# Layer one's weights shared by halves between the first two token blocks, and conversion work moved off GpSimd

## The chip, the core and the metric

The kernel runs on one core of one Trainium2 chip. The metric is device microseconds of one execution, the median of several. The engines are called TensorE (PE in the profile, PEld its weight loads), VectorE (DVE), ScalarE (ACT), GpSimd (POOL) and SyncE (SP, here the queue that issues every DMA).

## What is computed

A decayed linear attention (4 batches, 8 heads, 576 positions, head size 64) is followed by two feed-forward layers over 2304 tokens, 512 wide inside and 2048 in the middle. The weights come as float64, everything else as float32, and the products keep float32's digits.

```python
def _attn_ref(q, k, v):
    scores = np.matmul(q, k.transpose(0, 1, 3, 2)) / np.sqrt(64)
    Dmat = np.where(rel >= 0, gamma[:, None, None] ** rel[None, :, :], 0.0)
    return np.matmul(scores * Dmat[None], v)

def reference(**kwargs):
    x = attn_out.transpose(0, 2, 1, 3).reshape(2304, 512)
    h = x @ moe_w_in
    x = np.where(h > 0, h, np.exp(np.minimum(h, 0)) - 1) @ moe_w_out
    h = np.maximum(x @ moe2_w_in, 0)
    return (h * h) @ moe2_w_out
```

## The kernel before

**Products.** Every float32 operand is held as a pair of float32r parts, hi and lo. `split` (L99) makes the pair: ScalarE casts hi (L101) and a second engine subtracts to get lo (L102). `mm3` (L104) issues three matmuls for each product, hi by hi, hi by lo and lo by hi (L105 to L107).

**Blocks and steps.** The tokens go in five blocks, four of 512 and one of 256. A step is one block and one f of 16, that is 128 of the 2048 middle columns. `up` (L270) computes h in 12 matmuls into one of two PSUM banks, takes the nonlinearity in three ScalarE instructions and two VectorE ones (`t` at L287, the max at L288), and splits g. `down1` (L296) adds that f's share into four PSUM banks `acc`, 12 matmuls, and runs LAG = 2 steps behind. Layer one runs all 16 f of block zero, then of block one, and so on; layer two follows in the same manner, reading layer one's outputs back from DRAM.

**Weights.** A unit is 128 columns of w_in or 128 rows of w_out; a layer has 32 units, two for each f. `load_raw` (L112) fetches a unit's float64 words, 512 KB, into one of three buffers `raw`. `to_f32` (L124) makes float32 of them. ScalarE scales the lower words in place (L131) and takes the magnitude of the upper words (L132), VectorE does min (L133), shift (L134) and sign (L135), and GpSimd adds the rounded lower words (L138). `split_w` (L149) then makes the pair, with the subtraction on GpSimd for layer one's w_out and on VectorE otherwise. Layer one's pairs stay in SBUF, each under a tag of its own, through all five blocks. `w1_step` (L372) loads, splits and converts one unit per count; it is called once with each of the first block's attention pieces and twice in each step until all 32 units are done. From step 16 on, layer two's units are converted at 0.7 per step, parked in DRAM and fetched back in layer one's last block.

**Attention.** It runs by chunks of at most 128 positions: `transposes`, `scores`, `values`. `scale_chunk` (L179) multiplies q and k by their decays, on GpSimd for blocks zero and one and on VectorE for the rest. Block zero's four chunks come first, three of them in places of weights that come late. The attention of each later block is spread over the steps of the block ahead of it (`mid`, L404), since a block's first up-step needs its whole x.

**Order.** Each engine runs its instructions in the order that a scheduler fixes when the program is built. The scheduler takes what the program issues first, among what its own model holds ready. All DMAs go through SP's one queue, in order.

## Time and profile before

| what | value |
|---|---|
| median of 3 runs | 928.61 us (928.36 to 928.87) |
| span of the profiled execution, first to last instruction | 926.7 us |
| TensorE busy | 895.6 us, 97% |
| VectorE busy | 488.0 us, 53% |
| ScalarE busy | 420.5 us, 45% |
| GpSimd busy | 138.0 us, 15% |
| mean granted TensorE clock | 0.992 of full speed |

The profile shows one execution; its own time is the span, and the median of the runs is 1.9 us above it. Busy shares are averages over stages that differ much, so the stages have to be read apart: the attention of block zero (to about 35 us), the steps of block zero with the conversion of layer one's weights (to about 159 us), and all that follows. Busy times of matmuls overlap each other, since the ends of pipelined matmuls are modelled; a group's matmuls therefore add up to more than the time they took.

### The profile page before, as it was taken

How to read it: one execution, taken by the hardware profiler on the slowest of the kernel's cores; microseconds unless marked ns; L12 is line 12 of the kernel's file. 1: busy time of each engine (PE TensorE's matmuls, PEld its weight loads, DVE VectorE, ACT ScalarE, POOL GpSimd, SP SyncE). 2: the span in 40 equal slices, each digit the busy share in tenths (PEclk: the TensorE clock that was granted, in tenths of full speed). 3: DMA queues.
4: the chain of work that ended last, by engine and by line, in shares of the span. 5: the costliest groups of instructions: out<-in, count | busy, mean ns of one | idle time of the engine just before them, and what ended most of it. 6: DMA issues, size and time to landing. Idle time of an engine off the chain costs nothing.

```text
span 926.7 us, 12546 instructions
## 1 busy us (share of the span) xinstructions
PE 895.6 (97%) x4934; PEld 741.2 (80%) x4934; DVE 488.0 (53%) x784; ACT 420.5 (45%) x762; POOL 138.0 (15%) x102
## 2 busy tenths in 40 slices
PE   6988788999999999999999999999999999999997
PEld 4766566878888888999888888888888888988886
DVE  4799999676656655776566542232223222323222
ACT  4576676665556565665666532222222222222221
POOL 4565555121111111211000000000000000000000
PEclk9999999999999999999999999999999999999999
DMA  9752555274434533663443420030002002100001
GB/s 227 180 159 93 159 150 158 65 230 127 113 100 173 137 91 107 220 176 122 150 126 92 159 91 1 1 137 1 0 1 91 1 1 82 55 2 23 1 1 45
DMA packets 94778, 89.09 MB, mean 96 GB/s; under 512 B 59008, under 2 KB 77568, under 8 KB 94208
## 3 DMA queue, kind: packets, MB, share of 16 engines
q1 hardware_dynamic: 94720, 88.30, 32.2%
q8 instruction: 38, 0.62, 0.3%
q14 instruction: 20, 0.16, 0.1%
HBM read 65.74 MB, written 22.54 MB: 95 GB/s over the span
## 4 chain that ended last, share of the span: by engine, by line
PE 83%; DVE 11%; issue 2%; ACT 1%; DMA 1%; POOL 1%; SPq 0%; DVEq 0%; ACTq 0%
PE acc L105 13%; PE acc L106 13%; PE acc L107 13%; PE h L105 13%; PE h L106 13%; PE h L107 13%; DVE f L133 2%; DVE f L135 2%; DVE t L287 2%; PE ps_o L242 2%; DVE f L134 1%; PE ps_s L223 1%; PE ps_t L210 1%; PE ps_o L238 1%; DVE w L102 1%
## 5 line engine op out<-in xcount | busy, mean ns | idle before, releaser
L105 PE MATMUL h<-x,w 128*128 128x512 f32 (+1 forms) x640 | 238.3, 373 | 6.5 <-DVE t L288 5.8
L107 PE MATMUL h<-x,w 128*128 128x512 f32 (+1 forms) x640 | 237.8, 372 | 1.9 <-DVE w L102 1.9
L106 PE MATMUL h<-x,w 128*128 128x512 f32 (+1 forms) x640 | 237.1, 371 | 0.0
L292 DVE SCALAR_TENSOR_TENSOR t<-h,t 128x512 f32<-128x512 f32 (+1 forms) x80 | 51.1, 639 | 229.9 <-ACT t L290 229.9
L290 ACT ACTIVATE t<-h 128x512 f32<-128x512 f32 (+1 forms) x80 | 44.5, 556 | 237.1 <-PE h L107 237.1
L101 ACT CAST g<-t 128x512 fp32r<-128x512 f32 (+1 forms) x160 | 92.4, 578 | 128.0 <-DVE t L288 65.2
L105 PEld LDWEIGHTS h<-x,w 128*128 128x128 f32 x640 | 121.3, 190 | 29.8 <-ACT e L284 3.8
L102 DVE TENSOR_TENSOR g<-t,g 128x512 fp32r<-128x512 f32 (+1 forms) x160 | 108.7, 679 | 66.3 <-ACT g L101 59.4
L107 PEld LDWEIGHTS h<-x,w 128*128 128x128 f32 x640 | 121.2, 189 | 24.7 <-DVE w L102 4.4
L106 PEld LDWEIGHTS h<-x,w 128*128 128x128 f32 x640 | 121.4, 190 | 21.1 <-DVE x L102 0.4
L138 POOL TENSOR_TENSOR f<-f,raw 128x512 int32<-128x512 int32 x64 | 94.2, 1472 | 270.6 <-DVE f L135 186.1
L106 PE MATMUL acc<-g,w 128*128 128x512 f32 (+1 forms) x320 | 119.3, 374 | 2.5 <-DVE g L102 2.5
L105 PE MATMUL acc<-g,w 128*128 128x512 f32 (+1 forms) x320 | 116.8, 381 | 4.9 <-ACT g L101 4.8
L107 PE MATMUL acc<-g,w 128*128 128x512 f32 (+1 forms) x320 | 118.1, 370 | 0.0
L105 PE MATMUL acc<-w,g 128*128 128x512 f32 x288 | 112.2, 390 | 0.0
L106 PE MATMUL acc<-w,g 128*128 128x512 f32 x288 | 112.2, 390 | 0.0
L107 PE MATMUL acc<-w,g 128*128 128x512 f32 x288 | 111.6, 389 | 0.0
L287 DVE SCALAR_TENSOR_TENSOR t<-e,t 128x512 f32<-128x512 f32 (+1 forms) x80 | 60.0, 750 | 53.6 <-ACT t L285 53.1
L105 PEld LDWEIGHTS acc<-g,w 128*128 128x128 f32 x320 | 60.0, 190 | 16.9 <-ACT g L101 5.7
L283 ACT ACTIVATE t<-h 128x512 f32<-128x512 f32 (+1 forms) x80 | 44.3, 554 | 60.6 <-PE h L107 59.6
L106 PEld LDWEIGHTS acc<-g,w 128*128 128x128 f32 x320 | 60.5, 189 | 13.8 <-DVE g L102 4.0
L107 PEld LDWEIGHTS acc<-g,w 128*128 128x128 f32 x320 | 60.4, 189 | 10.1
(62 smaller groups left out, 954.8 us busy)
## 6 DMA issues: line engine op xcount, KB each, us to landing
raw<-in_moe_w_in_dram SPq DMA_DIRECT2D x32, 512.0 KB, 4.2
raw<-in_moe_w_out_dram SPq DMA_DIRECT2D x32, 512.0 KB, 3.6
x2s<-x SPq DMA_DIRECT2D x16, 512.0 KB, 3.3
w2s<-f SPq DMA_DIRECT2D x32, 256.0 KB, 2.3
f<-w2s SPq DMA_DIRECT2D x32, 256.0 KB, 2.7
x<-x2s SPq DMA_DIRECT2D x4, 2048.0 KB, 7.9
out_dram<-o SPq DMA_DIRECT2D x18, 256.0 KB, 2.1
q<-in_q_dram SPq DMA_DIRECT2D x13, 256.0 KB, 4.3
```

The costliest lines, as they stand in the source:

```text
L101: nc.scalar.copy(pair_hi, src)
L102: eng.tensor_tensor(out=pair_lo, in0=src, in1=pair_hi.bitcast(F32), op=ALU.subtract)
L105: nc.tensor.matmul(ps, l_hi, r_hi, start=first, stop=False)
L106: nc.tensor.matmul(ps, l_hi, r_lo, start=False, stop=False)
L107: nc.tensor.matmul(ps, l_lo, r_hi, start=False, stop=last)
L133: nc.vector.tensor_scalar_min(a, a, MOST)
L135: nc.vector.scalar_tensor_tensor(out=ai, in0=upper, scalar=-(1 << 31), in1=ai, op0=ALU.bitwise_and, op1=ALU.bitwise_or)
L138: nc.gpsimd.tensor_tensor(out=ai, in0=ai, in1=lower, op=ALU.add)
L283: nc.scalar.activation(t, h, AF.Relu, scale=-1.0)
L287: nc.vector.scalar_tensor_tensor(out=t, in0=e, scalar=1.0, in1=t, op0=ALU.add, op1=ALU.mult)
L290: nc.scalar.activation(t, h, AF.Relu)
L292: nc.vector.scalar_tensor_tensor(out=t, in0=h, scalar=0.0, in1=t, op0=ALU.max, op1=ALU.mult)
```

## The change

- **Halves.** Layer one's steps run in the order f 0 to 7 of block zero, f 0 to 7 of block one, f 8 to 15 of block zero, f 8 to 15 of block one, and then blocks two to four as before. A half's four sums are copied from PSUM to SBUF by ScalarE and written to DRAM (`parts`). At the end of the second half they are loaded back into raw buffers and added by VectorE before the split.
- **Spread.** The attention of block one now lies in steps 0 to 6, that of block two in steps 24 to 30.
- **Raw words.** Layer one's raw units load into the place that their pair will take, so each has a place of its own; `w1_step` issues loads up to six units ahead of the conversion. Layer two's still use the three `raw` buffers, which the halves' sums share.
- **GpSimd.** The rounding add and the split of layer one's w_out go to VectorE, and so does the scaling of block one's chunks. GpSimd keeps the scaling of block zero's chunks. The add is built as a custom VectorE instruction over 1024 half-words per partition.

Comments were taken out as well; those lines are left out of the diff.

```diff
+AHEAD = 6
+HALF = NF // 2
+ORDER1 = [(b, h * HALF + f) for h in range(2) for b in range(2) for f in range(HALF)]
+ORDER1 += [(b, f) for b in range(2, NB) for f in range(NF)]
+SPREAD = {1: (0, HALF - 1), 2: (3 * HALF, 4 * HALF - 1), 3: (2 * NF, 3 * NF - 3), 4: (3 * NF, 4 * NF - 3)}
...
+    parts = dram.tile([2, P, KC, TB], F32, tag="parts", name="parts")
...
-        t = raw_p.tile([P, DM, 2], I32, tag="raw", name="raw")
+        if layer == 0:
+            t = wp.tile([P, DM, 2], I32, tag=f"w{which}_{f}", name="raw")
+        else:
+            t = raw_p.tile([P, DM, 2], I32, tag="raw", name="raw")
...
-        nc.gpsimd.tensor_tensor(out=ai, in0=ai, in1=lower, op=ALU.add)
+        nc.vector.tensor_tensor(out=ai, in0=ai, in1=lower, op=ALU.add)
...
-        split(t[:, 0], t[:, 1], f32s.pop(u), nc.gpsimd if which and layer == 0 else nc.vector)
+        split(t[:, 0], t[:, 1], f32s.pop(u))
...
-        eng = nc.gpsimd if ch in blocks[0] + blocks[1] else nc.vector
+        eng = nc.gpsimd if ch in blocks[0] else nc.vector
...
+    def halves(blk):
+        return blk < 2
...
+        half = halves(blk)
+        first, last = f == 0 or half and f == HALF, f == NF - 1 or half and f == HALF - 1
+        if first:
             acc_t[blk] = [ps_acc.tile([P, TB], F32, tag="acc", name=f"acc{m}") for m in range(KC)]
+        if f == NF - 1 and half:
+            back = [raw_p.tile([P, 2, TB], F32, tag="raw", name="part") for _ in range(KC // 2)]
+            for i, t in enumerate(back):
+                nc.sync.dma_start(out=t, in_=parts[blk, :, 2 * i:2 * i + 2])
...
             if f == NF - 1:
+                if half:
+                    t = back[m // 2][:, m % 2]
+                    nc.vector.tensor_tensor(out=t, in0=a, in1=t, op=ALU.add)
+                    a = t
...
+            elif last:
+                if m % 2 == 0:
+                    part = raw_p.tile([P, 2, TB], F32, tag="raw", name="part")
+                nc.scalar.copy(part[:, m % 2], a)
+                if m % 2:
+                    nc.sync.dma_start(out=parts[blk, :, m - 1:m + 1], in_=part)
...
-            step("raw", 99, w1, lambda u: load_raw(*u))
+            while at["raw"] < min(at["f32"] + AHEAD, len(w1)):
+                step("raw", 99, w1, lambda u: load_raw(*u))
             step("split", at["f32"], w1, split_w)
-            step("f32", at["raw"] - 2, w1, to_f32)
+            step("f32", at["raw"], w1, to_f32)
...
-    steps = [(0, blk, f) for blk in range(NB) for f in range(NF)]
+    steps = [(0, blk, f) for blk, f in ORDER1]
...
+            for of, (lo, hi) in SPREAD.items():
+                if lo <= i < hi:
+                    need = 3 * len(blocks[of])
+                    for _ in range((i - lo + 1) * need // (hi - lo) - (i - lo) * need // (hi - lo)):
+                        attn_step()
...
-                while at["raw"] == len(w1) and at["f32"] < len(w1) and at["f32"] < 2 * i + 6:
-                    step("f32", 99, w1, to_f32)
```

The built order shows where the instructions now stand. First VectorE, in before: from one step's t to the next one's in the early part of block zero (`L287` t, `L288` max, `L133` to `L135` a conversion, `w_2` the split of a unit of f 2, `g` the split of a step's result).

```order
L287 SCALAR_TENSOR_TENSOR t<-e,t 128x512
L288 TENSOR_TENSOR t<-h,t 128x512
L102 TENSOR_TENSOR w_2_268<-f,w_2_268 128x512
L133 TENSOR_SCALAR f<-f 128x512
L102 TENSOR_TENSOR x<-ps_o,x 128x4x64
L134 TENSOR_SCALAR f<-f 128x512
L102 TENSOR_TENSOR g<-t,g 128x512
L135 SCALAR_TENSOR_TENSOR f<-raw,f 128x512
L287 SCALAR_TENSOR_TENSOR t<-e,t 128x512
L288 TENSOR_TENSOR t<-h,t 128x512
L133 TENSOR_SCALAR f<-f 128x512
L134 TENSOR_SCALAR f<-f 128x512
```

VectorE in the changed kernel, between the eighth step of block zero and the first step of block one (`L146` to `L148` and `ISA` at L151 are a conversion with its add, `L111` splits, `L239` and `L271` attention).

```order
L148 SCALAR_TENSOR_TENSOR f<-raw,f 128x512
L147 TENSOR_SCALAR f<-f 128x512
L151 ISA f<-raw,f 128x1024
L146 TENSOR_SCALAR f<-f 128x512
L148 SCALAR_TENSOR_TENSOR f<-raw,f 128x512
L147 TENSOR_SCALAR f<-f 128x512
L111 TENSOR_TENSOR w_12_1160<-f,w_12_1160 128x512
L151 ISA f<-raw,f 128x1024
L111 TENSOR_TENSOR x<-ps_o,x 128x4x64
L148 SCALAR_TENSOR_TENSOR f<-raw,f 128x512
L271 TENSOR_TENSOR st<-ps_u,st 64x4x64 x2
L146 TENSOR_SCALAR f<-f 128x512
```

In before each few conversions are followed by a step's t, max and g; in the changed kernel there is a stretch with conversions and attention alone, 74 instructions long, and the last split of block one's x (`x<-ps_o,x 128x4x64`) stands inside it.

TensorE in before, in the middle of block zero (`h` is an up-step, `acc` a down-step, `ps_t` the transposes of a chunk of the next block).

```order
L105 MATMUL acc_698<-g,w_5_550 128x512
L106 MATMUL acc_698<-g,w_5_550 128x512
L107 MATMUL acc_698<-g,w_5_550 128x512
L105 MATMUL h<-x,w_8_669 128x512
L106 MATMUL h<-x,w_8_669 128x512
L210 MATMUL ps_t<-cs,q 128x128 x4
L105 MATMUL acc_695<-g,w_6_613 128x512
L105 MATMUL acc_696<-g,w_6_613 128x512
L107 MATMUL h<-x,w_8_669 128x512
L105 MATMUL h<-x,w_8_669 128x512
```

TensorE in the changed kernel, at the end of block zero's first half.

```order
L115 MATMUL acc_762<-g,w_7_746 128x512
L116 MATMUL acc_762<-g,w_7_746 128x512
L115 MATMUL acc_763<-g,w_7_746 128x512
L116 MATMUL acc_763<-g,w_7_746 128x512
L223 MATMUL ps_t<-cs,q 128x128 x4
L223 MATMUL ps_t<-cs,k 128x128 x4
L236 MATMUL ps_s<-qT,kT 128x128 x8
L251 MATMUL ps_o<-qT,st 128x128 x4
L255 MATMUL ps_o<-P_999,v 64x128
L255 MATMUL ps_o<-P_1001,v 64x128
```

The last two chunks of block one's attention, whose pieces stood between the matmuls of block zero's steps, now follow the last matmuls of the half, with no step between them.

SP's queue in before, where layer one's last units are loaded (`raw` a unit, `q`, `k` and `v` a chunk of the next block).

```order
L175 DMA k<-in_k_dram 128x8x64
L175 DMA v<-in_v_dram 128x8x64
L116 DMA raw<-in_moe_w_in_dram 128x4x256
L175 DMA q<-in_q_dram 128x8x64
L121 DMA raw<-in_moe_w_out_dram 128x1024
L116 DMA raw<-in_moe_w_in_dram 128x4x256
L121 DMA raw<-in_moe_w_out_dram 128x1024 x2
L175 DMA k<-in_k_dram 128x8x64
L175 DMA v<-in_v_dram 128x8x64
L116 DMA raw<-in_moe_w_in_dram 128x4x256 x2
L121 DMA raw<-in_moe_w_out_dram 128x1024
```

SP's queue in the changed kernel, at the end of layer one's units.

```order
L134 DMA raw<-in_moe_w_out_dram 128x1024
L129 DMA raw<-in_moe_w_in_dram 128x4x256
L134 DMA raw<-in_moe_w_out_dram 128x1024
L129 DMA raw<-in_moe_w_in_dram 128x4x256
L134 DMA raw<-in_moe_w_out_dram 128x1024
L129 DMA raw<-in_moe_w_in_dram 128x4x256
L134 DMA raw<-in_moe_w_out_dram 128x1024
L188 DMA q<-in_q_dram 128x8x64
L188 DMA k<-in_k_dram 128x8x64
L188 DMA v<-in_v_dram 128x8x64
L188 DMA q<-in_q_dram 128x8x64
```

The chunks' loads and the units' took turns; now all units are issued ahead of the third chunk of block one.

## Rows read from the trace of the kernel before

**Rows 1.** The page, part 2: busy tenths in 40 slices of 23.2 us.

```profile
PE   6988788999999999999999999999999999999997
...
DVE  4799999676656655776566542232223222323222
```

**Rows 2.** Busy time by stage: us, then per engine busy us and instructions, clock, DMA.

```profile
42.00:100.00 58.00, 49.38 (x285) 36.43 (x284) 57.46 (x77) 40.66 (x73) 32.65 (x23) 1.00 0.50 142
100.00:158.80 58.80, 48.61 (x281) 37.18 (x279) 57.49 (x81) 39.88 (x73) 33.89 (x22) 0.93 0.54 148
158.80:921.90 763.10, 762.99 (x4046) 641.31 (x4046) 347.74 (x587) 320.17 (x585) 49.04 (x35) 1.00 0.26 82
```

**Rows 3.** TensorE groups, 0 to 158.8 us: group, count, busy, mean ns, idle before.

```profile
L105 PE MATMUL h<-x,w 128*128 128x512 f32 x61 | 25.6, 423 | 6.5 <-DVE t L288 5.8 <-ACT e L284 0.4 <-ACT t L283 0.2
...
L105 PE MATMUL acc<-g,w 128*128 128x512 f32 x52 | 18.4, 424 | 4.8 <-ACT g L101 4.8
```

**Rows 4.** TensorE alone, 660 to 760 us: us, busy and matmuls, clock, DMA.

```profile
660.00:760.00 100.00, 100.00 (x443) 1.00 0.06 21
```

**Rows 5.** VectorE groups by shape, 30 to 160 us; columns as in rows 3.

```profile
L134 DVE TENSOR_SCALAR f<-f 128x512 int32<-128x512 int32 x29 | 22.0, 761 | 0.3
L133 DVE TENSOR_SCALAR f<-f 128x512 f32<-128x512 f32 x30 | 21.6, 720 | 1.8 <-ACT f L132 1.7
L287 DVE SCALAR_TENSOR_TENSOR t<-e,t 128x512 f32<-128x512 f32 x14 | 16.4, 1174 | 0.1
...
L226 DVE TENSOR_TENSOR P<-ps_s,cs 128x512 f32<-128x512 f32 x6 | 3.9, 677 | 0.0
...
L226 DVE TENSOR_TENSOR P<-ps_s,cs 64x256 f32<-64x256 f32 x4 | 1.5, 407 | 0.0
```

**Rows 6.** The same view, 160 to 380 us.

```profile
L287 DVE SCALAR_TENSOR_TENSOR t<-e,t 128x512 f32<-128x512 f32 x34 | 24.6, 723 | 39.1 <-ACT t L285 39.1
...
L134 DVE TENSOR_SCALAR f<-f 128x512 int32<-128x512 int32 x25 | 10.5, 421 | 0.4
L133 DVE TENSOR_SCALAR f<-f 128x512 f32<-128x512 f32 x24 | 10.3, 430 | 0.6 <-ACT f L132 0.3 <-issue 0.2
```

**Rows 7.** VectorE in order of time: start us, duration us, instruction.

```profile
77.44 0.68 DVE L287 SCALAR_TENSOR_TENSOR t<-e,t 128x512 f32<-128x512 f32 x1
78.04 0.68 DVE L135 SCALAR_TENSOR_TENSOR f<-raw,f 128x512 int32<-128x512 int32 x1
...
80.96 0.42 DVE L134 TENSOR_SCALAR f<-f 128x512 int32<-128x512 int32 x1
81.30 1.78 DVE L102 TENSOR_TENSOR g<-t,g 128x512 fp32r<-128x512 f32 x1
```

**Rows 8.** VectorE's fourth x split, the first t and the fifteenth.

```profile
34.37 0.69 DVE L102 TENSOR_TENSOR x<-ps_o,x 128x512 fp32r<-128x512 f32 x1 [0.43 <-ACT x L101]
...
41.98 0.68 DVE L287 SCALAR_TENSOR_TENSOR t<-e,t 128x512 f32<-128x512 f32 x1
...
154.45 1.77 DVE L287 SCALAR_TENSOR_TENSOR t<-e,t 128x512 f32<-128x512 f32 x1
```

**Rows 9.** DMA, 0 to 30 us, in 40 slices of 0.75 us, and its mean.

```profile
GB/s 0 0 62 280 282 232 225 245 218 210 216 228 207 237 322 351 350 303 243 214 216 205 225 176 248 217 268 364 286 218 189 170 164 172 217 178 214 146 274 393
DMA packets 19038, 6.72 MB, mean 224 GB/s; under 512 B 17259, under 2 KB 18879, under 8 KB 19037
```

**Rows 10.** ScalarE in order of time: start us, duration us, instruction.

```profile
43.29 0.66 ACT L131 ACTIVATE raw<-raw 128x512 int32<-128x512 uint32 x1
43.84 0.66 ACT L132 ACTIVATE f<-raw 128x512 f32<-128x512 f32 x1
```

**Rows 11.** TensorE and its granted clock in stretches of 2 us.

```profile
104.00:106.00 2.00, 0.00 (x0) 1.00 0.14 23
...
108.00:110.00 2.00, 2.00 (x7) 0.50 0.79 223
...
158.00:160.00 2.00, 1.48 (x6) 0.50 1.03 284
```

More of the change, by code (lines that the diff above doesn't have):

```diff
@@ L298, in down1 @@
         g, w = g_t.pop((blk, f)), w_t[0, 1, f]
-        if f == 0:
+        half = halves(blk)
+        first, last = f == 0 or half and f == HALF, f == NF - 1 or half and f == HALF - 1
+        if first:
             acc_t[blk] = [ps_acc.tile([P, TB], F32, tag="acc", name=f"acc{m}") for m in range(KC)]
+        if f == NF - 1 and half:
+            back = [raw_p.tile([P, 2, TB], F32, tag="raw", name="part") for _ in range(KC // 2)]
+            for i, t in enumerate(back):
+                nc.sync.dma_start(out=t, in_=parts[blk, :, 2 * i:2 * i + 2])
         for m in range(KC):
@@ L303, in down1 @@
             a = acc_t[blk][m][:, :n]
-            mm3(a, w[:, 0, c], w[:, 1, c], g[:, 0, :n], g[:, 1, :n], f == 0, f == NF - 1)
+            mm3(a, w[:, 0, c], w[:, 1, c], g[:, 0, :n], g[:, 1, :n], first, last)
             if f == NF - 1:
+                if half:
+                    t = back[m // 2][:, m % 2]
+                    nc.vector.tensor_tensor(out=t, in0=a, in1=t, op=ALU.add)
+                    a = t
                 x2 = g_p.tile([P, 2, TB], F32R, tag="g", name="x2")[:, :, :n]
@@ L404, in mid @@
         def mid():
-            if layer == 0 and blk < NB - 1:
-                need = 3 * len(blocks[blk + 1])
-                for _ in range(min(need, (f + 1) * need // (NF - 3)) - min(need, f * need // (NF - 3))):
-                    attn_step()
+            for of, (lo, hi) in SPREAD.items():
[3 more added lines that the diff above has]
+                        attn_step()
             if at["split"] < len(w1):
                 w1_step(2)
-                while at["raw"] == len(w1) and at["f32"] < len(w1) and at["f32"] < 2 * i + 6:
-                    step("f32", 99, w1, to_f32)
             elif layer == 0 and i >= NF and at["f322"] < min(len(w2), (i - NF + 1) * 0.7):
```

## Prediction, made before the changed kernel had run

> **What bounds the kernel now.** I read the page's slices first, then busy time by stage, then the engines' groups inside the stage that is short. In the slices TensorE stands at 9 from the seventh slice to the end, and below that only ahead of it [rows 1]; VectorE stands at 9 in just that early stretch. By stage [rows 2]: from 42 to 158.8 us VectorE is busy 57.5 of 58 and 57.5 of 58.8 us, and TensorE is left with holes of 8.6 and 10.2 us; from 158.8 to 921.9 TensorE is busy 762.99 of 763.1 us. So whatever happens after 158.8 beside TensorE is free, and all there is to win or lose lies ahead of it: a stage in which VectorE converts layer one's 32 weight units while block zero runs. By 158.8 TensorE has issued 61 + 60 + 60 matmuls of up-steps and 3 × 52 of down-steps, 337 of 512 columns [rows 3]. Their pace when nothing waits is 100 us / 443 = 0.226 us [rows 4].
>
> Why is VectorE full? Its own work is not that large. Min, shift and the first step of t take 720, 761 and 1174 ns in that stage, against 430, 421 and 723 ns later, when GpSimd has little to do [rows 5, 6]. Times their counts (30, 29, 14) that is 8.7 + 9.9 + 6.3 = 25 us of waiting beside GpSimd's adds and splits. A second count agrees: undisturbed, a two-tensor instruction starts 0.60 us after the one before it (77.44 to 78.04), and what follows a shift 0.34 us after it (80.96 to 81.30) [rows 7]; with its waits I take 0.36, and 0.36 for the half-width ones. The 162 instructions from the first t (41.98) to the fifteenth (154.45) [rows 8] come to 81 us so priced and took 112.5.
>
> **Part 1: work leaves GpSimd.** GpSimd keeps only the scaling of block zero. This returns up to those 31 us to VectorE in the stage, and puts on it, for layer one, 32 adds, 16 splits of w_out and the scaling of block one's five chunks (10 instructions). Splits and scalings are two-tensor instructions of 512 words: 26 × 0.60 = 15.6 us. The add is a new form, shown in the built order as one instruction over 1024 half-words; the trace of before has none on VectorE. Lower bound: 0.60 us, that of a two-tensor instruction over the same 512 words with the same strided raw operand (the sign step, L135); nothing that reads two tensors is cheaper, so a gain is excluded. Upper bound, if each half-word takes a turn of its own: 256 words take 407 ns and 512 take 677 [rows 5], so 270 ns per 256 more, and 1024 come to 0.60 + 0.54 = 1.14 us. I take 0.60, the row of the same words and layout; 32 × 0.60 = 19.2 us (36.5 at the other end). So 34.8 us come and some 31 go: VectorE's total for the conversions stays where it was.
>
> [...]
>
> The same 32 adds for layer two (19 to 37 us) fall after 158.8, where VectorE is busy only 347.7 of 763.1 us [rows 2]: cost 0.
>
> **Part 2: halves.** The steps' new order runs f 0 to 7 of block zero, then f 0 to 7 of block one, so that 16 units would feed 16 steps. But w1_step(2) still stands in every step and the scheduler still places conversions where they become ready: in VectorE's queue 74 instructions (36.7 us: 23 min or shift, 12 sign, 11 adds, 10 splits and attention) stand between the g of the eighth step and the t of the ninth, where in before 8 to 15 instructions lie between one t and the next. And block one cannot begin before its x is complete, whose last split stands in the midst of them. TensorE then has only two chunks of attention to do. So the date that counts is that split's end, T1.
>
> VectorE's queue up to T1. In before the fourth chunk's x split starts at 34.37 and the first t at 41.98 [rows 8]. In the new order 6 adds and 3 more splits stand ahead of the first t, but the scaling of the fourth chunk no longer stands behind two adds on GpSimd. I let the two cancel and leave the x split's end at 35.4; 13 instructions follow it (8 at 0.60, 5 at 0.36: 6.6 us): first t at 42.0. From there to the last x split of block one stand 149 instructions: 81 of two tensors, 19 adds, 37 min or shift, 12 of half width, 60.0 + 13.3 + 4.3 = 77.6 us. That gives 119.6 if it never waits.
>
> It waits for two things. **Loads:** AHEAD and the places of their own let all 32 raw loads go without waiting for GpSimd to free a buffer, and in SP's queue all of them now stand ahead of q and k of block one's third chunk. 16.8 MB at the 303 to 351 GB/s that raw loads reach alone, and 5.05 MB of other loads at some 215 GB/s [rows 9]: 52 + 23.5 + 1.5 to start + 1.5 to land, 79 us, where VectorE comes to that chunk's scaling after 65 instructions, 34.4 us, at 76.4. **ScalarE:** its part of the conversions is pulled ahead: from the first t to the sixth x cast its queue holds 59 instructions, 32 us at 0.55 us from start to start [rows 10], and VectorE's queue 30 us up to the same place, and each hands work to the other. I put 5 us for both (0 to 12): **T1 = 124.6.**
>
> After T1: of 3456 matmuls in both layers (512 columns each) 192 are done against 337 in before at 158.8, so 145 × 0.226 = 32.7 us more are left; attention of block one is done in both. TensorE then runs two up-steps (5.4 us) and a piece of attention (2.2), and waits for the ninth step's max, 23 instructions or 11.6 us behind T1: 4 us. Where TensorE has paused some us it was granted half its clock for about 3.5 us (0.50 at 108 to 110 after 104 to 106 empty; again from 158 [rows 11]); one such stretch lies behind 158.8 as well, a second here costs 1.75. Sum: 124.6 + (926.7 − 158.8) + 32.7 + 4.0 + 1.75 = **931.0 us** of span. The median of the three runs stands 1.9 us above the profiled span of 926.7: **932.9 us**.
>
> **Costed at nothing:** 8 copies of partial sums on ScalarE (0.55), 8 adds on VectorE (0.60), 8 transfers of 512 KB to and from DRAM. The first half's four copies lie in the hole ahead of T1, the rest where TensorE is full and VectorE, as behind 158.8 in before, under half busy; without that cover 9.2 us. Each second read-back waits for a raw buffer that a layer-two conversion frees, and a PSUM bank waits for the read-back; TensorE has two up-steps (5.4 us) between, so I put 0 there, 0 to 4 into the range.
>
> **Rivals.**
> *B: the add costs 1.14.* For: the order's 1024 elements. Then the first t comes at 45.2 (6 × 0.54 later), the stretch takes 77.6 + 19 × 0.54 = 87.9, loads are hidden by that (wait 1), T1 = 134.1, and the wait behind T1 is 2 us longer: 942.5 + 1.9 = 944 us.
> *C: nothing waits, faster.* If the loads keep ahead and ScalarE's handoffs hide, T1 = 119.6; if the low clock lies inside the wait of 4 us rather than beside it, the end is 119.6 + 767.9 + 32.7 + 3 = 923.2 + 1.9 = 925 us. It decides for faster where the waits named above (5, 4 and 1.75 us) come to less than 4.6 us together.
> *D: the loads decide.* If raw and other loads share 230 GB/s, as the first 30 us did on average (224 [rows 9]), 21.9 MB land at 98 us, T1 = 98 + 43.2 = 141 and the time 950 us; at 270 GB/s 84 + 43.2 = 127 and 936. For: everything is asked for at once, which before never was. Against: two raw loads alone reached 350.
> *E: the halves do what they say*, TensorE going on from block zero to block one without a hole: the 18.8 us of holes [rows 2] go, 910 us. Against: the built order, which is fixed.
>
> **How the numbers follow.** Forecast A (half-word add as 512 words, T1 near 125): 0.54, own range 927 to 938. B 0.15, C 0.15, D 0.14, E 0.02. I predict A's 933. The range leaves out most of E, the far ends of D and C: 925 to 946. Within 0.2% (926.8 to 930.5, about what a measurement of this kernel can tell from no change) lies A's lower edge, 0.13, and a part of C, 0.04: 0.17. Faster are C's rest 0.11, E 0.02 and a little of A, 0.04: 0.17. Slower are B 0.15, D 0.14 and the greater part of A, 0.37: 0.66.
>
> **What would show it.** The add's mean duration, 0.68 or 1.2 us. GpSimd without work after some 25 us; min and shift at 0.42 where they were 0.72 and 0.76. A hole on TensorE between about 98 and 125 us, filled with two chunks of attention, ended by VectorE's x; VectorE full until then. From some 140 us on TensorE full to the end. I am wrong if TensorE has no such hole, if it waits later than 150 us, or if block one's x is complete before 115 or after 135.

## The result, and the profile of the changed kernel

The changed kernel is slower: 936.6 us, median of four runs (935.0 to 937.2), against 928.5 us for four runs of the kernel before; the ratio is 1.008 with a 95% interval of 1.0066 to 1.0095. The profiled execution spans 934.9 us, 8.2 us more than the 926.7 of before. The forecast was 933 us (925 to 946), with slower as the likeliest sign.

| | before | changed |
|---|---|---|
| span of the profiled execution | 926.7 us | 934.9 us |
| VectorE busy | 488.0 us | 503.0 us |
| GpSimd busy | 138.0 us | 9.3 us |
| fourth x split of block zero starts | 34.4 us | 38.3 us |
| first t | 42.0 us | 45.4 us |
| block one's x complete | 158.0 us | 125.3 us |

The page's slices of the changed kernel (part 2; they answer to [rows 1]):

```profile
PE   8799679999999999999999999999999999999997
...
DVE  5899997367866766788566632222222222323222
...
PEclk9799869999999999999999999999999999999999
```

The fifth and sixth slices (94 to 140 us) stand at 6 and 7 on TensorE, and the granted clock falls to 8 and 6 tenths with them: that is the hole. Busy time by stage, in the changed kernel (the stages of [rows 2]; us, then per engine busy us and instructions, granted clock, DMA):

```profile
42.00:100.00 58.00, 54.16 (x344) 43.70 (x343) 55.95 (x108) 48.62 (x89) 0.00 (x0) 0.97 0.66 201
100.00:158.80 58.80, 45.96 (x289) 37.37 (x288) 54.94 (x105) 32.45 (x60) 0.00 (x0) 0.80 0.35 92
158.80:930.00 771.20, 769.98 (x4036) 645.64 (x4034) 364.24 (x622) 322.69 (x588) 0.00 (x0) 1.00 0.26 82
```

TensorE lost 3.8 us in the first stage and 12.8 in the second (8.6 and 10.2 in before), the second at a mean clock of 0.80; behind 158.8 it is full again but for 1.2 us. Its idle time in the two stages is thus no longer than in before (16.6 against 18.8 us). What got done is less: by 158.8 us 285 matmuls of steps are out, where before had 337 [rows 3], with a chunk and a half of attention more; steps began later, and much of the second stage ran at half clock. So, but for those 1.2 us, nearly all was decided ahead of some 160 us, as in before.

VectorE's groups in the changed kernel, 30 to 160 us (busy, mean ns of one; they answer to [rows 5]):

```profile
L151 DVE CUSTOM_DVE_ANT_0 f<-raw,f 128x1024 uint16<-128x1024 uint16 x30 | 20.3, 684 | 0.0
...
L146 DVE TENSOR_SCALAR f<-f 128x512 f32<-128x512 f32 x29 | 12.2, 419 | 0.0
L147 DVE TENSOR_SCALAR f<-f 128x512 int32<-128x512 int32 x29 | 12.0, 419 | 0.1
L300 DVE SCALAR_TENSOR_TENSOR t<-e,t 128x512 f32<-128x512 f32 x13 | 8.9, 686 | 2.3 <-ACT t L298 2.3
```

The add over 1024 half-words takes 684 ns, as long as two-tensor instructions over 512 words (684 for the sign step at L148, 686 for t), and min, shift and t are back at 419, 419 and 686 ns (720, 761 and 1174 in [rows 5]). Now the hole, on TensorE in order of time (start us, us, instruction, idle time before it and what ended it):

```profile
100.50 0.39 PE L116 MATMUL acc<-g,w 128*128 128x512 f32 x1
100.73 0.60 PE L223 MATMUL ps_t<-cs,q 128*128 128x128 f32 x4
...
106.66 2.08 PE L251 MATMUL ps_o<-qT,st 128*128 128x128 f32 x8 [2.87 <-DVE P L239]
...
113.15 0.48 PE L223 MATMUL ps_t<-cs,q 64*128 64x64 f32 x4 [2.27 <-DVE x L111]
...
119.36 1.97 PE L251 MATMUL ps_o<-qT,st 128*128 128x64 f32 x8 [3.13 <-DVE P L239]
...
125.31 0.79 PE L115 MATMUL h<-x,w 128*128 128x512 f32 x1 [0.67 <-DVE x L111]
```

From 100.7, when block zero's first half is done, to 125.3 TensorE has two chunks of attention and the first two matmuls of block one, and VectorE releases each piece late: P and x stand between conversions. Behind it, stretches of the changed kernel, with the granted clock in the third column from the end:

```profile
126.00:128.00 2.00, 2.00 (x6) 1.55 (x5) 1.96 (x5) 0.28 (x1) 0.00 (x0) 0.50 0.36 68
...
132.00:134.00 2.00, 1.92 (x13) 1.46 (x11) 2.00 (x5) 2.00 (x5) 0.00 (x0) 1.00 0.00 0
...
138.00:140.00 2.00, 2.00 (x6) 1.60 (x5) 2.00 (x4) 0.68 (x1) 0.00 (x0) 0.50 0.00 0
```

```profile
125.30:141.50 16.20, 14.16 (x58) 11.22 (x59) 16.12 (x31) 9.85 (x18) 0.00 (x0) 0.73 0.25 53
141.50:932.00 790.50, 787.31 (x4133) 659.85 (x4132) 378.77 (x647) 332.55 (x605) 0.00 (x0) 1.00 0.26 82
```

TensorE starts block one at half clock (0.50), reaches the full one (1.00) at some 130, waits 2.0 us (1.3 for a piece of block two's attention, 0.7 for the ninth step's max) and falls to half clock (0.50) again until 141.

### The profile page after: what moved, and what is told of

Read it like the earlier page. It is cut to its first block, busy times and chain, and to the rows that moved or that the text cites. A ratio compares the mean times of both kernels' runs of the same rounds, so it can differ in the third digit from the quotient of the medians.

```text
span 934.9 us, 12416 instructions
## 1 busy us (share of the span) xinstructions
PE 903.4 (97%) x4934; PEld 751.9 (80%) x4934; DVE 503.0 (54%) x882; ACT 425.0 (45%) x770; POOL 9.3 (1%) x12
## 3 DMA queue, kind: packets, MB, share of 16 engines
q1 hardware_dynamic: 95872, 92.49, 32.5%
## 4 chain that ended last, share of the span: by engine, by line
PE 88%; DVE 9%; DMA 1%; issue 1%; ACT 0%; SPq 0%; DVEq 0%
PE acc L114 14%; PE h L114 14%; PE h L115 13%; PE acc L115 13%; PE h L116 13%; PE acc L116 13%; PE ps_o L255 2%; DVE f L148 1%; PE ps_s L236 1%; DVE f L151 1%; PE ps_o L251 1%; PE ps_t L223 1%; DVE w L111 1%; DVE f L146 1%; DMA v<-in_v_dram 1%
## 5 line engine op out<-in xcount | busy, mean ns | idle before, releaser
L111 DVE TENSOR_TENSOR g<-t,g 128x512 fp32r<-128x512 f32 (+1 forms) x160 | 101.8, 637 | 65.1 <-ACT g L110 58.6
L115 PE MATMUL acc<-g,w 128*128 128x512 f32 (+1 forms) x320 | 118.4, 371 | 1.1 <-DVE g L111 1.1
L116 PE MATMUL acc<-g,w 128*128 128x512 f32 (+1 forms) x320 | 118.1, 370 | 0.0
L114 PE MATMUL acc<-g,w 128*128 128x512 f32 (+1 forms) x320 | 112.4, 376 | 0.0
L300 DVE SCALAR_TENSOR_TENSOR t<-e,t 128x512 f32<-128x512 f32 (+1 forms) x80 | 50.9, 636 | 57.7 <-ACT t L298 57.3
L116 PEld LDWEIGHTS acc<-g,w 128*128 128x128 f32 x320 | 60.3, 188 | 10.2
L116 PEld LDWEIGHTS acc<-w,g 128*128 128x128 f32 x288 | 54.1, 188 | 11.3
```

Of the source, the lines that this page charges most:

```text
L111: eng.tensor_tensor(out=pair_lo, in0=src, in1=pair_hi.bitcast(F32), op=ALU.subtract)
L114: nc.tensor.matmul(ps, l_hi, r_hi, start=first, stop=False)
L115: nc.tensor.matmul(ps, l_hi, r_lo, start=False, stop=False)
L116: nc.tensor.matmul(ps, l_lo, r_hi, start=False, stop=last)
L300: nc.vector.scalar_tensor_tensor(out=t, in0=e, scalar=1.0, in1=t, op0=ALU.add, op1=ALU.mult)
```

## The experiments

The theory behind the forecast: conversions that block one doesn't need yet stand ahead of its x in VectorE's queue, and TensorE has nothing else to do meanwhile. The rivals tried below are that the engine moves, the raw places, the loads or the partial sums are what costs. The kernels ran beside the kernel before on several chips, whose medians for it went from 928.5 to 930.7 us, so ratios are to be compared across chips rather than times. The profiled execution of held_halfpace, halves_old_raw and held_scaling_gpsimd was the slowest of its kernel's ten or eleven, 5 to 9 us above the median: what its trace shows need not all be in the median.

| kernel | us | ratio to before, 95% interval |
|---|---|---|
| changed kernel | 936.6 | 1.0080 (1.0066 to 1.0095) |
| moved_alone | 918.6 | 0.9873 (0.9855 to 0.9891) |
| no_halves | 917.9 | 0.9848 (0.9817 to 0.9878) |
| halves_alone | 965.4 | 1.0376 (1.0360 to 1.0392) |
| halves_old_raw | 935.3 | 1.0051 (1.0029 to 1.0073) |
| moved_but_scaling | 916.9 | 0.9869 (0.9849 to 0.9889) |
| held_twopace | 939.1 | 1.0100 (1.0074 to 1.0126) |
| held_onepace | 931.1 | 1.0023 (1.0008 to 1.0038) |
| held_halfpace | 931.1 | 1.0020 (1.0003 to 1.0037) |
| held_scaling_gpsimd | 930.6 | 1.0007 (0.9990 to 1.0024) |
| held_early_loads | 938.3 | 1.0087 (1.0054 to 1.0121) |
| halves_old_raw_held | 919.6 | 0.9873 (0.9848 to 0.9899) |
| no_part_sums | 935.6 | 1.0062 (1.0043 to 1.0081) |

### The three parts, alone and in pairs

**Engine moves alone** (moved_alone): the kernel before with these three lines.

```diff
-        nc.gpsimd.tensor_tensor(out=ai, in0=ai, in1=lower, op=ALU.add)
+        nc.vector.tensor_tensor(out=ai, in0=ai, in1=lower, op=ALU.add)
...
-        split(t[:, 0], t[:, 1], f32s.pop(u), nc.gpsimd if which and layer == 0 else nc.vector)
+        split(t[:, 0], t[:, 1], f32s.pop(u))
...
-        eng = nc.gpsimd if ch in blocks[0] + blocks[1] else nc.vector
+        eng = nc.gpsimd if ch in blocks[0] else nc.vector
```

> The kernel before with part 1 alone: add, w_out split and the scaling of block one's chunks on VectorE, old order of steps, old raw buffers. Forecast's part 1 (what comes, 34.8 us, and the waits beside GpSimd that go, some 31, cancel): from the first t to the fifteenth VectorE holds 211 instructions, priced 111.0 us without waits, where before 162 took 112.5, so TensorE is full from some 157 to 163 us on and the time is 926 to 934 us. Rival W (the waits beside GpSimd were not what held VectorE, so they don't come back): up to 34.8 us slower, 950 to 963. Rival S (scaling on VectorE waits for its loads with the conversions queued behind it): 935 to 945.

It took 918.6 us, faster by 1.3%, 7 us below the lower end of what the theory gave. VectorE's last x split of block one and its fifteenth t, in moved_alone:

```profile
125.35 0.42 DVE L102 TENSOR_TENSOR x<-ps_o,x 128x256 fp32r<-128x256 f32 x1
...
158.40 0.69 DVE L287 SCALAR_TENSOR_TENSOR t<-e,t 128x512 f32<-128x512 f32 x1
```

and the fifteenth t in before:

```profile
162.85 0.68 DVE L287 SCALAR_TENSOR_TENSOR t<-e,t 128x512 f32<-128x512 f32 x1
```

The t at 154.45 in [rows 8], which the prediction took for the fifteenth, is the fourteenth, 150 instructions behind the first; the 162 instructions that it counted reach to 162.85. So from the first t to the fifteenth the 162 instructions of before took 120.9 us, not 112.5, and the waits beside GpSimd come to 120.9 − 81 = 40 us, not 31. In moved_alone the 211 took 117.9 us (first t at 40.49), 6.2 of them idle; priced were 111.0 without waits. The queue went as priced, then, and is some 3 us shorter than in before. TensorE gained more. Its groups in moved_alone up to 158.8 us, with the same columns as [rows 3]:

```profile
L105 PE MATMUL h<-x,w 128*128 128x512 f32 x62 | 25.2, 409 | 1.5 <-DVE t L288 1.1 <-ACT w L101 0.5
...
L105 PE MATMUL acc<-g,w 128*128 128x512 f32 x56 | 17.1, 421 | 3.1 <-ACT g L101 3.0
L223 PE MATMUL ps_s<-qT,kT 64*128 64x128 f32 (+1 forms) x128 | 11.1, 272 | 3.2 <-ACT kT L215 3.2
```

and the last of these in before, over the same time:

```profile
L223 PE MATMUL ps_s<-qT,kT 64*128 64x128 f32 (+1 forms) x96 | 6.3, 267 | 0.7 <-ACT kT L215 0.7
```

By 158.8 us 353 matmuls of steps are out against 337 [rows 3], and two more chunks of attention (128 score products against 96, 16 to a chunk). Block one's x is complete at 125.8 where in before it was at 158.0. So in before it was the attention too that came late: what moved_alone has done of block two's by then, TensorE in before has still to do when its holes have closed.

**The engine moves without the scaling** (moved_but_scaling) differs from moved_alone in one line and tells which move that was:

```diff
-        eng = nc.gpsimd if ch in blocks[0] else nc.vector
+        eng = nc.gpsimd if ch in blocks[0] + blocks[1] else nc.vector
```

> The kernel before with the add and the split of w_out on VectorE, and the scaling of block one's chunks left on GpSimd: the engine moves without the scaling. VectorE has 6 us less queued up to the fifteenth t (10 instructions of 0.60) and waits for no loads of k (2.6 us with all three moves); GpSimd, with nothing but scaling, does it as the loads land. Theory A (the adds and splits beside VectorE were what stretched it and held block one's attention): at least as fast as all three moves, 911 to 918 us. Rival B (it was the scaling, queued behind adds on GpSimd, whose move brought the gain, or its ten instructions stretch VectorE again): 919 to 926.

916.9 us, as theory A had it: it was adds and splits on GpSimd (which of the two was not tried), not the place of the scaling, and once GpSimd does nothing else the scaling can stay there. VectorE's last x split of block one in this kernel:

```profile
115.99 0.41 DVE L102 TENSOR_TENSOR x<-ps_o,x 128x256 fp32r<-128x256 f32 x1
```

It comes 9 us earlier than in moved_alone. The time is 1.7 us lower than that of moved_alone, but the two intervals overlap. Both beat both kernels of the study.

**Halves and raw places alone** (halves_alone): the changed kernel with the three lines above as they were in before.

> The changed kernel with add, w_out split and the scaling of block one back on GpSimd: halves and raw places alone. Up to block one's last x split VectorE holds 133 instructions from the first t, priced 65.2 us without waits (149 and 77.6 in the changed kernel). If GpSimd's adds and splits stretch them as in before (112.5 us for instructions priced 81), they take 90 us, the split ends at 44 + 90 = 134 us, and the time is 941 to 948. Rival (VectorE is not stretched there, or other engines decide): 65 to 75 us, split at 110 to 119 and 922 to 931.

965.4 us, far past the 941 to 948 expected. VectorE's groups in halves_alone, 30 to 160 us (busy, mean ns):

```profile
L147 DVE TENSOR_SCALAR f<-f 128x512 int32<-128x512 int32 x30 | 27.6, 922 | 0.5
L146 DVE TENSOR_SCALAR f<-f 128x512 f32<-128x512 f32 x30 | 26.4, 881 | 1.0 <-ACT f L145 0.9
...
L300 DVE SCALAR_TENSOR_TENSOR t<-e,t 128x512 f32<-128x512 f32 x8 | 9.7, 1207 | 0.0
...
L301 DVE TENSOR_TENSOR t<-h,t 128x512 f32<-128x512 f32 x8 | 5.4, 681 | 0.1
...
L239 DVE TENSOR_TENSOR P<-ps_s,cs 128x512 f32<-128x512 f32 x6 | 3.9, 681 | 0.0
```

The stretching beside GpSimd is stronger than in before (shift 922 ns against 761, min 881 against 720). Conversions now follow each other without a step between, and GpSimd is busy 62% of the time from the first t to block one's last x split against 57% in before; that this is the reason is not shown. That split ends at 153.6, with the first t at 49.4: 104.3 us for 133 instructions priced 65.2, a factor of 1.60. I had carried over 1.39, which rests on the miscounted t; with the 120.9 us that the 162 instructions of before took it is 1.49, and the split would have been expected at 141 rather than 134. The rows also show which instructions are stretched: min, shift and t, which have all their inputs in SBUF (881, 922 and 1207 ns, against 419, 419 and 686 in the changed kernel), and not the max and P, which read one input from PSUM (681 ns both, against 684 and 685 there). Why these and not those, no run shows.

**No halves** (no_halves): the changed kernel with the old order of steps.

```diff
-ORDER1 = [(b, h * HALF + f) for h in range(2) for b in range(2) for f in range(HALF)]
-ORDER1 += [(b, f) for b in range(2, NB) for f in range(NF)]
+ORDER1 = [(b, f) for b in range(NB) for f in range(NF)]
...
-SPREAD = {1: (0, HALF - 1), 2: (3 * HALF, 4 * HALF - 1), 3: (2 * NF, 3 * NF - 3), 4: (3 * NF, 4 * NF - 3)}
+SPREAD = {b + 1: (b * NF, (b + 1) * NF - 3) for b in range(4)}
...
-        return blk < 2
+        return False
```

> The changed kernel with the old order of steps, the old spread and no halves: raw places and the engine moves alone. VectorE's first t comes as late as in the changed kernel (45 us; 40.5 with the engine moves alone), and 201 instructions lie between the first and the fifteenth t (211 with the engine moves alone). Theory H (the order by halves is what turns the 918.6 us of the engine moves into 936.6: TensorE has only half of block zero to do until block one's x is there): 915 to 925 us. Rival P (the raw places, by their early loads and conversions, cost the 18 us): 930 to 938.

**Halves with the old raw buffers** (halves_old_raw): the changed kernel with

```diff
-        if layer == 0:
-            t = wp.tile([P, DM, 2], I32, tag=f"w{which}_{f}", name="raw")
-        else:
-            t = raw_p.tile([P, DM, 2], I32, tag="raw", name="raw")
+        t = raw_p.tile([P, DM, 2], I32, tag="raw", name="raw")
...
-            while at["raw"] < min(at["f32"] + AHEAD, len(w1)):
-                step("raw", 99, w1, lambda u: load_raw(*u))
+            step("raw", 99, w1, lambda u: load_raw(*u))
             step("split", at["f32"], w1, split_w)
-            step("f32", at["raw"], w1, to_f32)
+            step("f32", at["raw"] - 2, w1, to_f32)
```

and the lines after `w1_step(2)` that the change had taken out.

> The changed kernel with layer one's raw words in the three raw buffers, by the old rule of loading: engine moves and halves alone. First t at 40.5 as with the engine moves alone; from it to block one's last x split 129 instructions, priced 67.3 us (149 and 77.6 in the changed kernel), so that this split ends at 40.5 + 67.3 + 3 = 111 us, 14 us earlier. Theory P: most of the 18 us go, 919 to 925 us. Theory H: the hole ahead of block one stays, since TensorE has no other work there, 930 to 936.

no_halves took 917.9 us and halves_old_raw 935.3: by both times **theory H holds**, as long as conversions are issued at the changed kernel's pace (others follow below). With the engine moves in, the order by halves, together with its spread of attention and its partial sums, costs 2.3% with the raw places (0.9848 to 1.0080) and 1.8% with the old raw buffers (0.9873 to 1.0051), that is 17 to 22 us, and the raw places by themselves cost nothing that can be told. In no_halves TensorE loses 3 and 4 us in the stages in which the changed kernel loses 4 and 13 (here no_halves):

```profile
42.00:100.00 58.00, 54.98 (x319) 43.95 (x318) 56.04 (x108) 48.96 (x91) 0.00 (x0) 0.97 0.74 230
100.00:158.80 58.80, 54.94 (x374) 42.89 (x373) 58.48 (x112) 34.02 (x61) 0.00 (x0) 0.97 0.23 50
```

In halves_old_raw block one's last x split did end early, at 115.5, and yet little was won. The hole ahead of x did not simply stay, as theory H had it. TensorE's waits from 120 to 170 us there (total, times, longest), 12.4 us, where the changed kernel has 2.0 behind its x:

```profile
PE ps_s L233 <- ACT kT L225: 5.4, 2, 4.7
PE h L114 <- DVE t L298: 3.8, 2, 2.6
PE acc L114 <- ACT part L335: 3.2, 1, 3.2
```

With the raw words loaded later, fewer conversions lie ahead of x (129 instructions from the first t against 149) and more behind it, and it is block two's attention, block one's steps and, behind the copy of the sums, the next half's down-steps that wait.

### Fewer conversions ahead of block one's x

Three kernels differ from the changed one in `mid` alone. Conversions are issued behind the tanh of their step in ScalarE's queue, at two units per step as in the changed kernel (held_twopace), at one (held_onepace), and at half a unit in block zero's first half and five in four steps later (held_halfpace). The diff is that of held_halfpace; the other two have `w1_step(2)` and `w1_step(1)` behind the same `with`.

```diff
-                w1_step(2)
+                due = 12 + (i + 1) // 2 if i < HALF else 16 + 5 * (i + 1 - HALF) // 4
+                with tc.issue_after(mark[0]):
+                    while at["f32"] < min(due, len(w1)):
+                        w1_step(1)
+                    if due > len(w1):
+                        w1_step(1)
```

> The changed kernel with two units per step as it has them, but each held behind the tanh of its step, so that only the holding differs: 158 instructions, 82.1 us, up to block one's last x split. Theory Q: the split ends at 45.4 + 82.1 + 2 = 129.5 us, 4 us later than in the changed kernel, and the time is 939 to 943. Rival H (it is the holding that helps in the other two kernels, not the number of conversions ahead of x): faster than the changed kernel here too, below 930.

> As the half-pace kernel, but one unit per step all the way: 122 instructions, 64.3 us, between the first t and block one's last x split. Theory Q: the split ends at 45.4 + 64.3 + 2 = 112 us, the time is 916 to 922. Rival V: 930 to 938. Rival L: as the half-pace kernel.

> The changed kernel with layer one's conversions held back: from the first step on they stand in ScalarE's queue behind the tanh of their step, half a unit per step in block zero's first half and five in four steps after it. VectorE's queue from the first t to block one's last x split then holds 102 instructions, priced 54.2 us by the starts used in the forecast, where the changed kernel has 149 and 77.6 us. Theory Q (block one waits because conversions that it does not need stand ahead of its x in VectorE's queue): that split ends at 45.4 + 54.2 + 2 = 102 us (125.3 in the changed kernel), the wait and the two stretches at half clock behind it go too (3.3 + 4.1 us), so 906 to 912 us. Rival V (VectorE has too much work in all until some 150 us, wherever it stands): the waits come back at the later steps, 930 to 938. Rival L (loads and ScalarE decide when x is there): the split stays behind 115 us, 925 to 936.

| kernel | VectorE's queue, first t to block one's last x split | split ends, expected | measured | time expected (theory Q) | measured |
|---|---|---|---|---|---|
| held_twopace | 82.1 us | 129.5 | 130.7 | 939 to 943 | 939.1 |
| changed | 77.6 us | 124.6 | 125.3 | 927 to 938 | 936.6 |
| held_onepace | 64.3 us | 112 | 117.5 | 916 to 922 | 931.1 |
| held_halfpace | 54.2 us | 102 | 114.7 | 906 to 912 | 931.1 |

Theory Q is right about the direction and about the changed kernel's own hole: with more ahead of x it grows, with less it shrinks, and holding as such wins nothing. Its times for the two slower paces failed, by 9 and 19 us. Both results lie in the range of rival V (930 to 938), and that of held_halfpace in the range of rival L too (925 to 936, split behind 115; it ends at 114.7). V's waits at later steps are there in part: in held_halfpace's trace TensorE waits 6.0 us from 115 to 330 for t, g and w. And the queue stops deciding at some 115 us. In held_halfpace VectorE is idle for 11.6 of the last 19.6 us up to the split, and what is left is a chain. TensorE there:

```profile
92.73 1.05 PE L251 MATMUL ps_o<-qT,st 128*128 128x128 f32 x8
...
96.22 0.66 PE L223 MATMUL ps_t<-cs,q 128*128 128x128 f32 x4 [0.95 <-DVE x L111]
...
101.91 2.07 PE L251 MATMUL ps_o<-qT,st 128*128 128x128 f32 x8 [1.65 <-DVE P L239]
...
107.22 0.46 PE L223 MATMUL ps_t<-cs,q 64*128 64x64 f32 x4 [0.95 <-DVE x L111]
...
114.62 1.22 PE L114 MATMUL h<-x,w 128*128 128x512 f32 x2
```

Each chunk's transposes begin when VectorE has split the x of the chunk before, and a chunk goes to and fro between TensorE, ScalarE and VectorE for 11 us (the fifth, half as long, for 7.4), much of it at half clock (0.50 from 100 to 104 and from 110 to 116).

Of the 10.6 us that held_halfpace was ahead at the split, its median kept 5.5. In the profiled execution, which kept nothing of it (span 934.6), VectorE waited for a load, with the next step's t behind it:

```profile
274.46 0.69 DVE L198 TENSOR_TENSOR k<-k,cs 64x512 f32<-64x512 f32 x1 [3.22 <-DMA k<-in_k_dram]
281.25 0.68 DVE L198 TENSOR_TENSOR q<-q,cs 64x512 f32<-64x512 f32 x1 [5.50 <-DMA q<-in_q_dram]
281.86 0.68 DVE L300 SCALAR_TENSOR_TENSOR t<-e,t 128x512 f32<-128x512 f32 x1
```

Two kernels tried to win that back. held_scaling_gpsimd has `eng = nc.gpsimd` for every chunk:

> The half-pace kernel with the scaling of every block's chunks on GpSimd. In the half-pace kernel VectorE waited for the loads of q and k in its own queue (2.8 us between 96 and 101, 5.5 + 5.2 us between 270 and 320), with a step's t and g behind; 9 of the 10 us that it had won by block one were lost between 280 and 312. Theory S (that queueing is where the gain went): TensorE has no waits of over 1 us between 270 and 320 and the time is 917 to 924. Rival R (the read-back of the halves' sums or TensorE's chain of attention loses them there): 928 to 933.

930.6 us: theory S falls, and the time lies in the range of rival R (928 to 933). The scaling no longer waited in VectorE's queue, but the first t had come later (49.8 us against 46.2), and TensorE then waited, as R has it, for the halves' sums, read back through the raw buffers (held_scaling_gpsimd, an execution of 939.9 us):

```profile
249.95 0.80 PE L114 MATMUL acc<-g,w 128*128 128x512 f32 x1 [2.70 <-DVE part L330]
```

held_early_loads, besides, lets four of block one's chunks load into places of late weights, ahead of the second half's raw words; lines that load three chunks ahead and keep the raw loads at 15 units until block one's attention is issued are left out here:

```diff
-    aside = blocks[0][1:4]
+    aside = blocks[0][1:4] + blocks[1][4:] + blocks[1][1:4]
...
```

> As the kernel with all scaling on GpSimd, and four of block one's chunks load into places of late weights, as three of block zero's do, ahead of the raw words of the second half's units; those are then loaded from the eighth step on. Theory L (what is left of the hole ahead of block one is the late start of its third chunk, loaded behind all raw words): block one's last x split ends before 106 us and the time is 4 to 9 us below the kernel with the scaling alone, 910 to 917. Rival (the chunks wait for each other's PSUM banks and cross VectorE and ScalarE in turn, whenever their loads come): within 2 us of it.

938.3 us, 8 us above the kernel with the scaling alone: theory L falls as well, and so does its rival, which had the two within 2 us. Block one's last x split ended at 115.5, 5 us earlier than there (expected: before 106), and the time was lost again elsewhere; where, I did not settle.

**Held, with the old raw buffers** (halves_old_raw_held): the edit of halves_old_raw, and in `mid`

```diff
-                w1_step(2)
+                due = 11 + 3 * i // 4 if i < HALF else 17 + 5 * (i + 1 - HALF) // 4
+                with tc.issue_after(mark[0]):
+                    while at["f32"] < min(due, len(w1)):
+                        w1_step(1)
...
```

> As the kernel with halves and the old raw buffers, and from the first step on the conversions stand behind the tanh of their step in ScalarE's queue, three quarters of a unit per step in block zero's first half and five in four steps after it: 107 instructions, 56.5 us, from the first t to block one's last x split, which ends at 40.5 + 56.5 + 3 = 100 us if VectorE decides it. Then 905 to 914 us. Rival C (the chain of the last chunks' attention decides it, as in the half-pace kernel with 7 to 11 us for a chunk, and the waits behind it come back): split at 108 to 116 and 918 to 926.

919.6 us, rival C by its numbers: the split ends at 108.1, not 100. This is the best that the halves gave here, 16 us below halves_old_raw, and still no better than the engine moves without halves (the intervals of 0.9873 and 0.9873 lie on each other). Two things follow that I had not looked for. So held, the order by halves costs nothing that can be told against moved_alone: the 17 to 22 us are the price of halves with conversions issued as in the changed kernel, not of the order as such. And the raw places, which cost nothing that can be told without holding, do cost with it: held_halfpace and held_onepace, with 102 and 122 instructions ahead of x where this one has 107, stay at 1.0020 and 1.0023, 1.5% or 14 us above. Why is not shown; nor was holding tried in the old order of steps, so what it is worth there is open.

### The partial sums

no_part_sums leaves out the copies, the transfers and the adds.

> The changed kernel without the halves' sums: the first half's sums of blocks zero and one are neither copied nor written to DRAM nor read back and added (the first half of layer one's middle columns is left out of those two blocks' result). Forecast: these copies, transfers and adds cost nothing, 935 to 938 us. Rival: they cost up to 9.2 us where nothing covers them, down to 927.

935.6 us, ratio 1.0062 against 1.0080 for the changed kernel, with intervals that overlap: what was costed at nothing can't be told from nothing here, and costs 4 us at most.

## Why the prediction came out, step by step

- **What bounds.** Right: VectorE ahead of some 140 us, TensorE behind.
- **The add (rival B).** Right: 684 ns, and the instruction behind it starts 0.60 us later (39.47, then 40.07). That it would cost what 512 words do was an estimate from the sign step, which takes 684 ns as well (L148); the trace of before, without such an add, did not decide between that and 1.14 us.
- **Part 1, "VectorE's total for the conversions stays where it was".** Right for VectorE within 3 us (117.9 us against 120.9), by luck in part: the miscounted t made the waits that go 31 us where they were 40, and moved_alone's queue waits 6.2 us again. It was wrong as a reading of what the part is worth: alone it makes the kernel 1.3% faster. The final sum did not go through this step, since it was built from the changed kernel's own queue, so the time came out. The split between the parts did not: the moves bring some 12 us and the halves cost 17 to 22, where the text let it seem as if moves brought nothing and halves cost 4. That the two sums ended near each other is luck as far as the parts go.
- **The start.** Mis-sized by 3.4 us: the first t at 45.36 instead of 42.0. "I let the two cancel" failed: the fourth x split came 3.9 us later than in before (38.26, 34.37 in [rows 8]). TensorE waited 2.9 us, until 32.5, for the update of the attention's state, which stood behind two P and two conversion instructions in VectorE's queue, and then ran at a mean clock of 0.61 until 40. With the engine moves alone the first t came at 40.5, with halves and the old raw buffers at 42.8 and 44.3, and in the runs with raw places at 43.4 to 49.8. VectorE in the changed kernel, with the add on which rival B was decided:

```profile
38.26 0.69 DVE L111 TENSOR_TENSOR x<-ps_o,x 128x512 fp32r<-128x512 f32 x1
...
39.47 0.69 DVE L151 CUSTOM_DVE_ANT_0 f<-raw,f 128x1024 uint16<-128x1024 uint16 x1
40.07 0.42 DVE L146 TENSOR_SCALAR f<-f 128x512 f32<-128x512 f32 x1
...
45.36 0.68 DVE L300 SCALAR_TENSOR_TENSOR t<-e,t 128x512 f32<-128x512 f32 x1
```

- **T1.** 125.3 us against 124.6. The stretch from the first t took 79.9 us where 77.6 of work and 5 of waits were put; VectorE waited 2.2 us, 1.8 of them for ScalarE and none for a load. The two errors, start and waits, cancel: that T1 came out within 0.7 us is luck.
- **Loads (rival D).** No wait: VectorE came to the scaling of block one's third chunk at 82.0 without idling. The sum's 1.5 us to land had no row behind it; in before the 256 KB writes of the parked weights landed 2.3 us after their issue (median), the transfer included.
- **Behind T1.** 809.6 us against 806.4. The waits came to 2.0 us instead of 4.0, and half clock took more: over 125.3 to 141.5 the mean clock is 0.73, that is 16.2 × 0.27 = 4.4 us. The sum holds 3.0 for it, the 1.75 and 1.2 in the stretch taken over from before (a mean clock of 0.80 from 158.8 to 165). A further 1.2 us of TensorE's time went between 285 and 295, at block two's start. These three come to 0.6 us of the 3.2; the rest I have not found.
- **Rival C**, 925 us, would have needed the waits below 4.6 us in all; they were 2.2, 2.0 and 3.2 (4.4 less the 1.2 of before) with a start 3.4 us late.
- **Rival E** (halves do what they say) was given 0.02. Even with pace, hold and old raw buffers the best was 919.6.
- **What would show it.** GpSimd without work from 22.4 us on, min and shift at 0.42, the hole from 100.7 to 125.3, TensorE full from 141.5: as written, but for one wait. The prediction calls itself wrong if TensorE waits later than 150 us, and it does once, for a step's max (the changed kernel):

```profile
294.11 0.50 PE L114 MATMUL h<-x,w 128*128 128x512 f32 x1 [1.08 <-DVE t L301]
```

  At 1.1 us of 934.9 it does not touch the account, but the sign was drawn too tightly.

Why the halves cost so much can be counted. By 125.3 us, when both have block one's x, moved_alone has issued 45 + 45 + 44 + 3 × 40 = 254 matmuls of steps and the changed kernel 34 + 32 + 32 + 3 × 32 = 194. The 60 that are missing are 13.6 us at 0.226; the waits and the half clock behind 125.3 are another 6.4, those at block two's start 1.2, and moved_alone waits 1.6 us behind 125.3 for its part. That makes 19.6, against 19.1 between the two spans. The groups in the changed kernel up to 125.3 us:

```profile
L114 PE MATMUL h<-x,w 128*128 128x512 f32 x34 | 14.9, 450 | 0.9 <-DVE t L301 0.7 <-ACT x L110 0.2
...
L115 PE MATMUL acc<-g,w 128*128 128x512 f32 x32 | 12.9, 404 | 1.1 <-DVE g L111 1.1
```

In the old order block zero has eight more steps for the time in which VectorE works on block one's attention. The halves put them behind block one.

What stays open: where the time goes in held_early_loads, why the raw places cost once conversions are held back, and why held_halfpace keeps only half of its lead in the median (its ten runs lie between 927.8 and 936.4 us, wider than those of the kernel before).

## What to carry to other kernels

When a stage is bound by a helper engine, price a change by the consumer's progress (matmuls issued by a fixed time), not by the helper's total: here VectorE's total changed by 3 us and the span by 11. Before weights are shared between blocks to halve their due dates, look at what the second block needs before it can start: an order that lets each unit serve two blocks also takes away the work that hid the second block's preparation. And move the parts one at a time: the three kernels with the engine moves and without halves (917 to 919 us, ratios 0.985 to 0.987, which can't be told apart) are faster than the whole change by some 2%.

## What the runs showed of the hardware

- The 32-bit integer add on VectorE, built over 1024 half-words, took 684 ns in the changed kernel, where the sign step, a two-tensor instruction over 512 words, took 684 as well.
- Waiting beside GpSimd was not a fixed price for each GpSimd instruction: shift took 761 ns in before and 922 in halves_alone, with the same adds, splits and scalings on GpSimd (busy 57% and 62% of the time from the first t to block one's last x split), and 419 in the changed kernel, without the adds and splits.
- TensorE at half clock inside the hole made the hole's own chain longer: in the changed kernel the eight products of a chunk with the state (`ps_o` at 106.66) took 2.08 us at a granted clock of 0.50, where held_halfpace at full clock (1.00 from 92 to 94; `ps_o` at 92.73) had 1.05.
